# Talking-heads attention and a squared-ReLU layer: the loads of v tied to later pre-mixings, more idle multiplications early, a new order of TensorE's work

## The chip, the cores and the metric

The kernel runs on one core of a Trainium2 chip. TensorE (PE in the profile) multiplies matrices and writes PSUM; ScalarE (ACT) and VectorE (DVE) read PSUM and write SBUF; GpSimd (POOL) does some of the elementwise work and issues the loads from and the stores to device memory; SyncE (SP) issues copies from SBUF to SBUF. The metric is the device time of one execution in microseconds, the median of several runs; smaller is better.

## The reference

Eight batches of 12 heads, 448 positions, head dimension 64. Scores of all heads are mixed across heads before the softmax, the probabilities are mixed across heads again after it, and the result goes through a two-layer network with relu squared:

```python
scores = scale * np.matmul(q, k.transpose(0, 1, 3, 2))
scores = np.einsum('bhij,hg->bgij', scores, w_pre)
scores = scores - np.max(scores, axis=-1, keepdims=True)
attn = np.exp(scores)
attn = attn / (np.sum(attn, axis=-1, keepdims=True) + 1e-09)
attn = np.einsum('bhij,hg->bgij', attn, w_post)
attn_out = np.matmul(attn, v)                      # 8 x 12 x 448 x 64
x = attn_out.transpose(0, 2, 1, 3).reshape(8 * 448, 768)
out = np.square(np.maximum(x @ w_in, 0.0)) @ w_out # 768 -> 2048 -> 768
```

The kernel takes the softmax without subtracting the maximum; the scores of these inputs are small.

## The kernel before, in words

Each batch goes through a pipeline, and the pipelines of neighbouring batches overlap.

- **Loads.** q and k of the next batch come in twelve DMAs of 112 KB (`load_qk`, line 659), v of a batch in six DMAs of 128 KB (`load_v`, line 670). POOL issues them, in one queue with its own elementwise work and the stores of results.
- **Transposes** (`emit_T`, line 762): q and k are turned on TensorE and put into `qkt`.
- **Scores** (`emit_QK`, line 905): a batch has four tiles of query rows, 128 rows each and 64 in the last. A unit of TensorE work multiplies for one pair of heads (for two pairs in the last tile, whose units are numbered 0, 2, 4); ACT and DVE copy each result from PSUM into `stage`. `stage` has two buffers, so a tile's copies wait until all of the tile two before it has been moved out of its buffer.
- **Moves** (`emit_rel`, line 951): SP sends rows of `stage` to `dring`, ten query rows with all 12 heads (120 partitions) to a slot. This brings the heads of one query row together in the partition dimension. There are 16 slots; a batch has 46 of these chunks. A slot is free when the pre-mixing of its old chunk is done.
- **Pre-mixing** (`emit_pre`, line 974): one unit mixes two chunks over the heads by a small weight matrix. ACT takes the exponential into `pring` (line 991, with row sums), DVE the reciprocal (1005), POOL folds it into the second mixing's weights (`wk2s`, 1012) and into a piece of the probabilities (`ptail`, 1027).
- **Post-mixing** (`emit_post`, lines 1057 and 1072): mixes again and transposes at once; ACT and DVE copy into `a2t`.
- **AV** (`emit_AV`, line 1138): the product with v in two halves of the query rows; it needs all six loads of v. Its result `xt` feeds F1 (`emit_F1`, 1217; 1189 for batches 0 and 1), relu and square (1245, 1246, 1255), and F2 (`emit_F2`, 1334; 1283 for the last tiles), whose results POOL stores (1366).

Of batch 0 the first 240 query rows take another way, without moves (lines 835 and 861).

What runs when is settled at build time by a planner (`_Plan.run`). TensorE's order is written out by hand as the string `ORDER`: each digit takes the next unit of one of ten streams (0 transposes, 1 QK, 2 pre-mixing, 3 post-mixing, 4 AV, 5 the way of batch 0, 6 and 7 F1, 8 and 9 F2). The other engines' orders come out of the planner, which takes ready tasks by assumed costs. A load takes a pair of numbers (`dma=("load", 870.0, 60.0)`: an assumed length, and an assumed measure of how far it holds up a move), used by the planner only. A load may also be tied by `after` to a task: the planner gives it out no sooner than that task. No semaphore comes of it: on the chip POOL issues the load when it has done what stands ahead of it in its own order.

Early in the program the planner also fills gaps of TensorE with multiplications whose result nobody reads (`warm_up`, line 628): for each gap it foresees, it puts in as many as fit into a share `WSHARE` of the gap (at the very start into another share).

The ties of v before:

```python
after = [qk_tasks[(1, 2)][-1]] if b < 1 else [pre_at(b * NCP + 8 + 2 * n)]
```

`n` counts the six loads, `NCP` is 46, `pre_at` gives the pre-mixing of a chunk. So the first load of a batch is tied to the pre-mixing of its chunk 8, the last to that of chunk 18. The loads of q and k are tied to chunks 2, 4, ... 24 of the batch before theirs.

Of the kernel before, what the change touches and what calls it, by code (L numbers as in the profile page):

```python
# [25 lines left out]
DMA_END = {"move": 3700.0, "load": 2300.0}  # L26
INF = float("inf")
ORDER = (
    "0011000011000011100000000000000005550000155001531515551555335553335533255003555001335214"
    "2142114123367372262366623331721716233776331167137242244321167611376632137772226632676217"  # L30
    "7333392293093902181238213832444026702181008111813381318312772266622316267117733633262422"
    "3443317711622676311761300276223833832281383127771266730027622008338111811183324242239119"
    "3319113922291933392432422443191161136220072371263363362126711773376220063732722008118113"
    "8221819333911393119224422281833381338222444422163161173372261163733370220611637327220062"
    "1637337229010911391319222818331831182224422933931393139122442248111812433812286313630027"
    "3272263363732173621637212763362007317022091391119133922244422181183338111833822281444382"
    "2286136373227600617117163336372217622673370022882118383009313911193119222444229139131933"
    "1922283811833382224442226361713736222671376131671373362126721379223938338219938382224442"
    "2868338367686376736722276776738338444867667767676677679989998898899"
)  # L40


# [302 lines left out]
def bass_talking_heads_attention__then__ffn_squared_relu_kernel(  # L345
# [38 lines left out]
    NCP = NCH + 1  # L384
# [7 lines left out]
    with ExitStack() as es:  # L392
# [12 lines left out]
        NWP = 4  # L405
        NSUB = 2
        WARM = 60000
        WSHARE = 0.6
        WPRIO = -700.0
        WC = FH  # L410
        ident = sb("ident", [128, 128], DT.bfloat16)
# [204 lines left out]
        def warm_up(gap):  # L616
            now = plan.free[PE]
            if now > WARM or not t_warm.done:
                return
            n = int((gap - 100.0) * (0.42 if now < 6000.0 else WSHARE) / 190.0)  # L620
            if n < 1 or plan.find(1, now)[0] > now + gap:
# [27 lines left out]
        qk_tasks, v_of, av_of, f1_of, f2_of = {}, {}, {}, {}, {}  # L649
# [16 lines left out]
        def load_v(b, u, h0, deps, after, prio):  # L666
            def fn(eng, en):
                i_ = bass.AP(v.tensor, (b * H + h0) * S * D + u * (NT - NS) * D,
                             [[NT * D, PJ], [S * D, 4], [1, NS * D]])
                eng.dma_start(vraw[64 * u:64 * u + 64, h0:h0 + 4, 1 - u:1 - u + NS, :],  # L670
                              i_).then_inc(sem_v.handle, 16)

            return plan.add("ldv%d_%d_%d" % (b, u, h0), POOL, fn, deps, {POOL: (610.0, 0.0)},
                            prio, sem_v, 16, after=after,
                            dma=("load", 870.0, 60.0))

        w_of = {}
        chain = {"t": None}
# [45 lines left out]
        def emit_load_v(b):  # L724
            ts = []
            for n, (h0, u) in enumerate((h0, u) for h0 in range(0, H, 4) for u in range(2)):
                after = [qk_tasks[(1, 2)][-1]] if b < 1 else [pre_at(b * NCP + 8 + 2 * n)]
                ts.append(load_v(b, u, h0, [last_av.get(b - 1)], after,
                                 -701.0 if b == 0 else b * 1000.0 - 1600.0))
            v_of[b] = ts  # L730

        def pre_at(g):
            return pre_of[g - g % NCP + g % NCP // 2 * 2]
# [644 lines left out]
        for b in range(B):  # L1378
# [29 lines left out]
            if b == 0:  # L1408
                emit_load_w(1, [dir_done[c] for c in range(ND)])
                emit_load_v(b)  # L1410
            else:
                emit_load_v(b)
# [85 lines left out]
```

## Time and profile before

| | |
|---|---|
| median of three runs | 530.37 us (529.73 to 532.08) |
| the profiled execution, its own time | 527.85 us |
| its span on the core | 526.0 us |
| TensorE busy | 506.4 us |
| ACT, DVE, POOL busy | 436.6, 405.5, 265.3 us |
| moves from `stage` to `dring` | 365 DMAs |
| loads of v | 48 DMAs of 128 KB |

The page gives busy time by engine, the span in 40 slices, the DMA queues, the chain of work that ended last, and groups of instructions. The trace answers narrower questions: windows of time, waits by releaser, the instructions of one tile, the timeline. A busy TensorE in the profile is not TensorE at its peak, since the ends of matmuls are modelled; its idle time is the surer reading.

### The profile page before, as it was taken

The page shows a single profiled execution, that of the slowest core. Times are in us where ns is not written, and L with a number is a line of the kernel's source. Part 1 is how long each engine was busy: PE and PEld are TensorE (multiplying, and loading weights), DVE is VectorE, ACT ScalarE, POOL GpSimd, SP SyncE. Part 2 cuts the span into 40 slices and gives each one's busy share as a digit, 9 for nine tenths or more (in the row PEclk, how much of TensorE's full clock was granted, in tenths as well). Part 3 has the DMA queues.
Part 4 walks back from the last instruction along what each step waited for, and adds up shares of the span by engine and source line. Part 5 has one row for each costly group of instructions (what it writes and reads, how often), then busy time and mean ns, then how long its engine had stood idle before and what let it go on. Part 6 is the DMA issues. An engine that isn't in the chain of part 4 may idle for free.

```text
span 526.0 us, 22045 instructions
## 1 busy us (share of the span) xinstructions
PE 506.4 (96%) x8923; PEld 314.1 (60%) x8923; DVE 405.5 (77%) x1066; ACT 436.6 (83%) x1248; POOL 265.3 (50%) x571
## 2 busy tenths in 40 slices
PE   8999989999989997999979999999999999999997
PEld 3456666667756653566535665566556665568874
DVE  7989977889979787977967779986797668965440
ACT  4999988899999897989979999997889888966421
POOL 9937449335843494246643478335843356242100
PEclk9999999999999999999989999999999999999999
DMA  8999989757975699447974679646974567453004
GB/s 112 207 223 196 205 162 185 174 107 143 175 179 107 143 174 192 84 91 157 170 150 79 129 154 197 136 78 143 186 143 98 129 136 141 86 99 78 4 19 103
DMA packets 83064, 72.02 MB, mean 137 GB/s; under 512 B 7572, under 2 KB 80468, under 8 KB 82964
## 3 DMA queue, kind: packets, MB, share of 16 engines
q0 software_dynamic: 37632, 33.83, 39.9%
q1 hardware_dynamic: 45044, 36.59, 30.2%
q8 instruction: 72, 1.18, 0.9%
q10 hardware_dynamic: 288, 0.20, 0.1%
q14 instruction: 28, 0.23, 0.1%
HBM read 47.22 MB, written 11.01 MB: 111 GB/s over the span
## 4 chain that ended last, share of the span: by engine, by line
PE 67%; DMA 12%; ACT 9%; DVE 7%; SPq 2%; POOL 2%; issue 1%; ACTq 0%; DVEq 0%; POOLq 0%
PE ps L1334 21%; PE ps L1217 18%; DMA dring<-stage 10%; PE ps L974 6%; PE ps L1189 5%; PE ps L1138 5%; ACT pring L991 5%; PE ps L1057 5%; PE ps L905 4%; DVE stage L482 3%; PE ps L1283 2%; SPq L951 2%; DMA kraw<-in_k_dram 2%; ACT stage L481 1%; PE ps L762 1%; DVE a2t L482 1%
## 5 line engine op out<-in xcount | busy, mean ns | idle before, releaser
L991 ACT ACTIVATE pring<-ps 128x448 bf16<-128x448 f32 x360 | 192.8, 572 | 7.6 <-PE ps L974 6.4
L1334 PE MATMUL ps<-w_out_sb,h2t 64*128 64x384 bf16 x1664 | 151.6, 323 | 0.3 <-DVE a2t L482 0.3
L1012 POOL TENSOR_TENSOR wk2s<-wk2b,rinv 128x120 bf16<-128x120 bf16 (+1 forms) x179 | 70.8, 396 | 141.8 <-DVE rinv L1005 140.7
L482 DVE CAST a2t<-ps 128x420 bf16<-128x420 f32 (+1 forms) x201 | 121.2, 639 | 18.2 <-PE ps L1072 17.3
L1217 PE MATMUL ps<-xt,w_in_sb 64*128 64x448 bf16 (+2 forms) x1344 | 123.2, 325 | 3.4 <-ACT stage L481 2.9
L482 DVE CAST stage<-ps 128x448 bf16<-128x448 f32 (+1 forms) x180 | 107.5, 614 | 24.5 <-DMA dring<-stage 12.9
L481 ACT ACTIVATE a2t<-ps 128x420 bf16<-128x420 f32 (+1 forms) x167 | 100.6, 662 | 17.3 <-PE ps L1072 16.7
L481 ACT ACTIVATE stage<-ps 128x448 bf16<-128x448 f32 (+1 forms) x180 | 94.9, 562 | 18.5 <-PE ps L905 10.6
L1334 PEld LDWEIGHTS ps<-w_out_sb,h2t 64*128 64x128 bf16 x1664 | 77.1, 94 | 50.2 <-issue 2.0
L1217 PEld LDWEIGHTS ps<-xt,w_in_sb 64*128 64x128 bf16 x1344 | 61.3, 94 | 43.2 <-ACT stage L481 3.1
L991 ACT ACTIVATION_READ_ACCUMULATOR pring<-ps 128x1 f32 x360 | 85.4, 237 | 0.0
L1366 POOL DMA_DIRECT2D out_dram<-osb x52 | 33.5, 648 | 100.7 <-ACT pring L991 43.4
L1027 POOL TENSOR_TENSOR ptail<-pring,rinv 128x128 bf16<-128x128 bf16 x171 | 70.3, 411 | 0.0
L1057 PEld LDWEIGHTS ps<-wk2s,pring 60*128 60x128 bf16 x2160 | 47.1, 94 | 25.3 <-issue 2.7
L1057 PE MATMUL ps<-wk2s,pring 60*128 60x60 bf16 x2160 | 54.3, 187 | 2.1 <-POOL ptail L1027 0.7
L1255 DVE TENSOR_TENSOR h2t<-h1t 128x448 bf16<-128x448 bf16 (+2 forms) x176 | 55.0, 340 | 1.4 <-ACT h1t L1245 1.0
L905 PE MATMUL ps<-qkt 64*128 64x448 bf16 (+1 forms) x360 | 50.2, 354 | 5.9 <-DVE h1t L1246 2.6
L974 PE MATMUL ps<-dring,wk 64*64 64x448 bf16 (+1 forms) x672 | 54.0, 365 | 1.9 <-ACT pring L991 1.1
L1246 DVE TENSOR_SCALAR h1t<-ps 128x448 bf16<-128x448 f32 (+2 forms) x92 | 43.7, 482 | 13.6 <-PE ps L1217 9.8
L1245 ACT ACTIVATE h1t<-ps 128x448 bf16<-128x448 f32 (+2 forms) x84 | 38.2, 466 | 11.6 <-PE ps L1217 10.0
L1005 DVE RECIPROCAL rinv<-rowsum 128x2 f32<-128x2 f32 (+1 forms) x184 | 28.5, 155 | 22.3 <-ACT pring L991 21.2
L1138 PEld LDWEIGHTS ps<-a2t,vraw 128*64 128x64 bf16 x960 | 38.8, 109 | 7.0 <-ACT osb L481 2.7
(66 smaller groups left out, 534.5 us busy)
## 6 DMA issues: line engine op xcount, KB each, us to landing
dring<-stage SPq DMA_DIRECT2D x307, 105.0 KB
out_dram<-osb POOLq DMA_DIRECT2D x52, 192.0 KB, 4.2
vraw<-in_v_dram POOLq DMA_DIRECT2D x48, 128.0 KB, 5.7
qraw<-in_q_dram POOLq DMA_DIRECT2D x48, 112.0 KB, 5.6
kraw<-in_k_dram POOLq DMA_DIRECT2D x48, 112.0 KB, 4.8
w_in_sb<-in_moe_w_in_dram POOLq DMA_DIRECT2D x8, 384.0 KB, 20.7
w_out_sb<-in_moe_w_out_dram POOLq DMA_DIRECT2D x8, 384.0 KB, 19.6
dring<-stage SPq DMA_DIRECT2D x30, 42.0 KB
```

What stands on the lines that cost most here:

```text
L481: return eng.activation(o, i_, AF.Copy)
L482: return eng.tensor_copy(o, i_)
L905: r_ = eng.matmul(ps[y * w:(y + 1) * w, g.banks[x], 0:S], qkt[r0:r0 + 64, pb, p + y, 0, i0:i0 + w], qkt[r0:r0 + 64, pb, p + y, 1, :], star ...
L974: r_ = eng.matmul(ps[64 * y:64 * y + 64, gr.banks[x], 0:S], wk1[64 * x:64 * x + 64 - R0 * x, :], dring[64 * x:64 * x + 64 - R0 * x, (g0 + ...
L991: return eng.activation(pring[:, pr, 0:S], ps[:, gr.banks[x], 0:S], AF.Exp, accum_out=rowsum[:, pr, :])
L1012: return eng.tensor_tensor(wk2s[:, p0:p0 + n, :], i0.to_broadcast([128, n, PR]), rinv[:, p0:p0 + n, :].to_broadcast([128, n, PR]), ALU.mult)
L1027: return eng.tensor_tensor(ptail[:, p0 // 2, :, :], pring[:, p0:p0 + 2, 0:PJ], rinv[:, p0:p0 + 2, :].to_broadcast([128, 2, PJ]), ALU.mult)
L1057: r_ = eng.matmul(ps[:, gr.banks[x], o0:o0 + PR], pring[64 * x:64 * x + PR, pr + y, (2 * k + 1) * PJ:(2 * k + 3) * PJ], wk2s[64 * x:64 * x ...
L1138: r_ = eng.matmul(po, vraw[:, h, sl, :], m, start=(k == 0), stop=(k == NS))
L1217: r_ = eng.matmul(ps[:, g.banks[x], 0:n], w_in_sb[64 * y:64 * y + 64, ft, t * 128:(t + 1) * 128], xt[64 * y:64 * y + 64, ft, c0:c1], start ...
L1255: return eng.tensor_tensor(h2t[:, t16, o0:o0 + n], h1t[:, s, 0:n], h1t[:, s, 0:n], ALU.mult)
L1334: r_ = eng.matmul(ps[:, g.banks[hh], 0:FH], h2t[64 * y:64 * y + 64, t16, col:col + 128], w_out_sb[64 * y:64 * y + 64, t16, hh * FH:(hh + 1 ...
```

## The change

Four edits. `WSHARE` goes from 0.6 to 0.85. The measure by which the planner lets a load of v hold up a move goes from 60 to 88, the number that the loads of q and k have. For batches 2 to 7 the six loads of v are tied to the pre-mixings of chunks 14, 17, 20, 23, 26 and 29 (an odd chunk stands for the pair that it is in), in place of 8, 10, ... 18; batches 0 and 1 keep theirs. And `ORDER` is another string with as many of each digit.

```diff
 ORDER = (
-    "0011000011000011100000000000000005550000155001531515551555335553335533255003555001335214"
-    "2142114123367372262366623331721716233776331167137242244321167611376632137772226632676217"
...
+    "0010000110100011010000155500000000001155355531155055500003305055300555333520055311135352"
+    "2441141233622673376262236133772111761376333127673222444213666761377111632236722677126332"
...
-        WSHARE = 0.6
+        WSHARE = 0.85
...
             return plan.add("ldv%d_%d_%d" % (b, u, h0), POOL, fn, deps, {POOL: (610.0, 0.0)},
                             prio, sem_v, 16, after=after,
-                            dma=("load", 870.0, 60.0))
+                            dma=("load", 870.0, 88.0))
...
             for n, (h0, u) in enumerate((h0, u) for h0 in range(0, H, 4) for u in range(2)):
-                after = [qk_tasks[(1, 2)][-1]] if b < 1 else [pre_at(b * NCP + 8 + 2 * n)]
+                after = [qk_tasks[(1, 2)][-1]] if b < 1 else [
+                    pre_at(b * NCP + (8 + 2 * n if b < 2 else 14 + 3 * n))]
```

No instruction of the computation is added or taken away; TensorE gets 27 idle multiplications for 23. What moves is shown at three places. Lines below the last edit have a number higher by one in the changed kernel.

**POOL in batch 4.** Rows of POOL's order from the fold of chunks 8 and 9 on (before), which bring four of the batch's six loads of v (line 670) among loads of batch 5's q and k (659) and the folds of chunks 10 to 13 (1012, 1027):

```order
L670 DMA vraw<-in_v_dram 64x4x256
L659 DMA qraw<-in_q_dram 64x2x448
L670 DMA vraw<-in_v_dram 64x4x256
L659 DMA qraw<-in_q_dram 64x2x448
L1012 TENSOR_TENSOR wk2s<-wk2b,rinv 128x120
L1027 TENSOR_TENSOR ptail<-pring,rinv 128x128
L1012 TENSOR_TENSOR wk2s<-wk2b,rinv 128x120
L1027 TENSOR_TENSOR ptail<-pring,rinv 128x128
L670 DMA vraw<-in_v_dram 64x4x256
L659 DMA kraw<-in_k_dram 64x2x448
L670 DMA vraw<-in_v_dram 64x4x256
L659 DMA kraw<-in_k_dram 64x2x448
```

Ahead of these rows stands one load of v after the fold of chunk 3, behind them the sixth after that of chunk 17. Now the first two loads of v stand behind the fold of chunks 12 and 13:

```order
L670 DMA vraw<-in_v_dram 64x4x256
L659 DMA kraw<-in_k_dram 64x2x448
L670 DMA vraw<-in_v_dram 64x4x256
L659 DMA kraw<-in_k_dram 64x2x448
L1013 TENSOR_TENSOR wk2s<-wk2b,rinv 128x120
L1028 TENSOR_TENSOR ptail<-pring,rinv 128x128
L1013 TENSOR_TENSOR wk2s<-wk2b,rinv 128x120
L1028 TENSOR_TENSOR ptail<-pring,rinv 128x128
L659 DMA qraw<-in_q_dram 64x2x448
L670 DMA vraw<-in_v_dram 64x4x256
L659 DMA qraw<-in_q_dram 64x2x448
L670 DMA vraw<-in_v_dram 64x4x256
```

The next two come after the fold of chunk 17, and the last two together after that of chunk 25. Ahead of the fold of chunk 15 stood five of the six loads before, and stand two now. The loads of q and k keep their places within a pair or two of chunks. The same holds for the other batches from 2 on; in batch 3 four of six are out by the fold of chunk 21, in batch 2 four by that of chunk 19, where all six were by 17 and 13 before. In batch 7 the last two come after the fold of chunk 25.

**TensorE at the last query tile of batch 3** (905 and 906 are the QK units, 4 matmuls each; 1217 and 1218 F1 of batch 2; 974 pre-mixing). Before, from the first QK unit of that tile on:

```order
L905 MATMUL ps<-qkt 64x448 x4
L974 MATMUL ps<-dring,wk 64x448 x4
L1217 MATMUL ps<-xt,w_in_sb 128x448 x24
L905 MATMUL ps<-qkt 64x448 x8
L1217 MATMUL ps<-xt,w_in_sb 128x448 x24
L1057 MATMUL ps<-wk2s,pring 128x60 x12
L1072 MATMUL ps<-wk2b,ptail 128x60 x2
```

The second and third unit stand together. Now, from the F1 unit ahead of the second QK unit to the third:

```order
L1218 MATMUL ps<-xt,w_in_sb 128x448 x12
L906 MATMUL ps<-qkt 64x448 x4
L975 MATMUL ps<-dring,wk 64x448 x4
L1218 MATMUL ps<-xt,w_in_sb 128x448 x24
L763 MATMUL ps<-ident,qkr 128x64 x28
L1218 MATMUL ps<-xt,w_in_sb 128x448 x12
L1058 MATMUL ps<-wk2s,pring 128x60 x12
L1073 MATMUL ps<-wk2b,ptail 128x60 x2
L1218 MATMUL ps<-xt,w_in_sb 128x448 x12
L1058 MATMUL ps<-wk2s,pring 128x60 x12
L1073 MATMUL ps<-wk2b,ptail 128x60 x2
L906 MATMUL ps<-qkt 64x448 x4
```

Between the second and the third now stand four F1 units of 12 matmuls, two transposes, a pre-mixing and two post-mixings. At the same place of batch 4 the order of the F1, QK and post-mixing units is what it was.

**TensorE at the start** (628 are the idle multiplications, 775 and 776 transposes, 835 and 836 the way of batch 0). Before, from the second group of idle multiplications on:

```order
L628 MATMUL ps<-warm 128x448 x3
L775 MATMUL ps<-ident,kraw 64x64 x28
L628 MATMUL ps<-warm 128x448
L905 MATMUL ps<-qkt 128x448 x4
L835 MATMUL ps<-qkt 32x448 x8
L775 MATMUL ps<-ident,qraw 64x64 x28
L628 MATMUL ps<-warm 128x448
L775 MATMUL ps<-ident,kraw 64x64 x28
```

Now:

```order
L628 MATMUL ps<-warm 128x448 x4
L776 MATMUL ps<-ident,kraw 64x64 x28
L628 MATMUL ps<-warm 128x448 x2
L906 MATMUL ps<-qkt 128x448 x2
L836 MATMUL ps<-qkt 32x448 x8
L776 MATMUL ps<-ident,qraw 64x64 x28
L628 MATMUL ps<-warm 128x448 x3
L776 MATMUL ps<-ident,kraw 64x64 x28
```

The three groups grow by one, one and two; a QK unit of 2 moves behind the second pair of transposes.

More of the change, by code (lines that the diff above doesn't have):

```diff
@@ L28 @@
 ORDER = (
-    "0011000011000011100000000000000005550000155001531515551555335553335533255003555001335214"
-    "2142114123367372262366623331721716233776331167137242244321167611376632137772226632676217"
[L31 to L39, printed above, removed]
+    "0010000110100011010000155500000000001155355531155055500003305055300555333520055311135352"
+    "2441141233622673376262236133772111761376333127673222444213666761377111632236722677126332"
+    "7733393912290293802381283213444200762180018111812383338316712267122266116732167337332244"
+    "4213673117612267611672330076722277383128338133832671006226722008338111811183324242239119"
+    "1119313933292229339242244324319116311622007317332622366321637127700736312672237800138122"
+    "8318119133913391192224422813833183318222424442236136173117326116733372200611637327022062"
+    "1637337229100913391119222818313833182224422933911193319322442224438113813183228631160022"
+    "7372263363372217623637211763063072372200931931191119222444223811831183138338222814443382"
+    "2287163367226116001731716333672127622637337002183821289318300911191139222444229139319333"
+    "9222818118333812244422261637133716222667337336171371612267221792183933822938339382224442"
+    "2833836768687736372226767637673384448678667676776767679989988988999"
 )
```

## The prediction

> **What bounds the kernel now.** First the page: which engine has the least idle time, and whether the clock drops.
>
> ```profile
> span 526.0 us, 22045 instructions
> PE 506.4 (96%) x8923; PEld 314.1 (60%) x8923; DVE 405.5 (77%) x1066; ACT 436.6 (83%) x1248; POOL 265.3 (50%) x571
> PEclk9999999999999999999989999999999999999999
> ```
>
> TensorE is idle for 526.0 - 506.4 = 19.6 us, some of it at the two ends, where nothing can be multiplied yet or any more. So a change that leaves the multiplications as they are can win some 15 us at most. One slice shows a lower clock.
>
> Next the end, since a stall that is taken away early is worth its length only if no other limit waits later. From 462 to 523 us:
>
> ```profile
> 462.00:523.00 61.00, 60.41 (x1010) 44.54 (x1004) 26.11 (x81) 28.23 (x83) 12.70 (x27) 1.00 0.27 59
> ```
>
> TensorE is busy for 60.4 of 61 us while ACT and DVE are idle for more than half. It has a backlog there, so a microsecond won in batches 2 to 6 reaches the end whole, and one lost does too.
>
> Third the waits of TensorE between 100 and 436 us, with total, times and longest, and the places on the timeline:
>
> ```profile
> PE ps L1217 <- ACT stage L481: 2.9, 1, 2.9
> PE ps L905 <- DVE h1t L1246: 2.6, 1, 2.6
> PE ps L974 <- ACT pring L991: 1.1, 1, 1.1
> PE ps L905 <- DVE a2t L482: 0.4, 2, 0.2
> ...
> 146.06 0.38 PE L974 MATMUL ps<-dring,wk 64*64 64x448 bf16 x4 [1.06 <-ACT pring L991]
> ...
> 206.24 0.38 PE L905 MATMUL ps<-qkt 64*64 64x448 bf16 x4 [2.63 <-DVE h1t L1246]
> 206.90 0.38 PE L905 MATMUL ps<-qkt 64*64 64x448 bf16 x4 [0.28 <-DVE stage L482]
> ...
> 266.94 2.42 PE L1217 MATMUL ps<-xt,w_in_sb 64*128 64x448 bf16 x12 [2.94 <-ACT stage L481]
> ```
>
> Three stalls, in batches 2, 3 and 4, all beside the last query tile (the units of 64 rows), make up 6.9 us; no other wait reaches half a microsecond. The named releasers, ACT and DVE, are only the last link. The chain of waits at the three places says what they waited for:
>
> ```profile
> 141.58 7.16 DMA dring<-stage
> ...
> 194.60 1.14 PE ps L1217 x12
> ...
> 196.44 8.51 DMA dring<-stage
> ...
> 259.03 6.11 DMA dring<-stage
> ```
>
> From the end of their issue these moves took 6 to 8.5 us to land. A copy into `stage` stands in ACT's and DVE's in-order queues until the tile two before is out of its buffer, so the copies behind it, which free PSUM for TensorE, stand too. The last of the three costs more than its idle time: the unit after it took 2.42 us, where the same 12 matmuls otherwise take 1.14, and the windows show why.
>
> ```profile
> 200.00:210.00 10.00, 6.95 (x88) 2.97 (x86) 6.56 (x17) 7.01 (x18) 3.89 (x8) 1.00 0.88 192
> 266.00:268.00 2.00, 1.06 (x6) 0.43 (x8) 1.94 (x4) 1.93 (x5) 0.00 (x0) 0.72 0.99 157
> 268.00:270.00 2.00, 2.00 (x26) 0.98 (x22) 0.86 (x3) 1.21 (x4) 0.00 (x0) 0.50 0.94 186
> 270.00:274.00 4.00, 4.00 (x72) 1.79 (x68) 3.42 (x10) 3.87 (x14) 1.64 (x4) 0.96 0.57 138
> ```
>
> From the means, half clock lasted 2 x 0.28/0.5 + 2 + 4 x 0.04/0.5 = 3.4 us, which loses 1.7 us of work. So batch 4's stall is worth 2.9 + 1.7 = 4.6 us. Batch 3's left the clock at 1.00.
>
> **The loads of v** (batches 2 to 7). Ten microseconds around 195, where batch 3's moves were late:
>
> ```profile
> q0 software_dynamic: 1596, 1.24, 79.2%
> vraw<-in_v_dram POOLq DMA_DIRECT2D x5, 128.0 KB, 6.5
> ```
>
> POOL's queue took 79.2% of the DMA engines for 10 us to move 1.24 MB: 7.9/1.24 = 6.4 us a MB, so a load of v (0.128 MB) is worth about 0.8 us of all 16 engines. They are taken from the moves of a tile, 13 of them, that run at the same time. By the orders shown, before its stall batch 4 now has three loads fewer to wait behind (two instead of five), batches 3 and 2 two fewer each.
>
> *Batch 4*: TensorE's order at the place is unchanged, so only the loads act. Three loads are 2.4 us of the 2.94; if that shortens the stall, the half clock should mostly go as well. I take 2.4 for the idle time and 1.0 of the 1.7, a gain of 3.4; bounds 0 (the moves wait for something else) and 4.6.
> *Batch 3*: two loads are 1.6 us, and the third QK unit now stands four F1 units (12 matmuls, 1.14 us each) further back, which by itself covers more than the 2.6 us if the wait comes at that unit. It may come at the second, so I take 2.5; bounds 0 and 2.9.
> *Batch 2*: two loads are 1.6 us against 1.06 of stall, but the order there was rewritten as well and I can't tell its slack: 0.5; bounds 0 and 1.1.
>
> [...]
>
> **What the loads meet later.** The load work isn't less, it comes 6 to 11 chunks later. These are the windows it goes into:
>
> ```profile
> 190.00:200.00 10.00, 10.00 (x206) 5.24 (x202) 9.43 (x23) 9.49 (x28) 9.61 (x20) 1.00 1.07 189
> 210.00:220.00 10.00, 10.00 (x207) 5.65 (x201) 9.20 (x26) 9.23 (x28) 2.44 (x6) 1.00 0.48 91
> ...
> 320.00:330.00 10.00, 10.00 (x184) 5.38 (x180) 9.43 (x25) 9.53 (x29) 7.80 (x17) 1.00 1.06 205
> 330.00:340.00 10.00, 10.00 (x170) 4.87 (x166) 9.87 (x26) 9.72 (x28) 3.08 (x8) 1.00 0.58 133
> ```
>
> The last numbers but one are the DMA share: 1.07 at the peak of batch 3, 0.48 and 0.58 in the stretch after the loads. Two to four loads of 0.8 us bring such a stretch to between 0.64 and 0.9, under the level at which moves were late; and batch 5 shows 1.06 with no stall at all, so a high share does not always bite. But the moves of that stretch fill the tile that the next batch's first query tile waits for. I take 2.0 us lost over the six batches, two stalls like batch 2's; bounds 0 and 9.2 (two like batch 4's).
>
> **AV** waits for the last load. Time from issue to landing of v in batches 5 to 7, and of F2's units:
>
> ```profile
> DMA to landing us min/median/max: 3.0/5.2/8.1
> ...
> 220.58 1.30 PE ps L1334 x16
> ```
>
> In batch 7, which has the least room, the last two loads follow the fold of chunk 25. From that pair's pre-mixing to AV TensorE's order has seven F2 units (9.1 us) and some 3 us of smaller ones; exponentials and fold take about 3 of the 12. The 9 that are left are more than the longest landing, 8.1. So 0; bounds 0 and 3. Behind a late AV would stand everything of TensorE.
>
> **The idle multiplications.** Four more, in gaps that the trace shows:
>
> ```profile
> 7.32 0.81 PE L628 MATMUL ps<-warm 128*128 128x448 bf16 x3
> 8.06 0.41 PE L775 MATMUL ps<-ident,kraw 64*64 64x64 bf16 x28
> ...
> 9.14 0.55 PE L905 MATMUL ps<-qkt 64*128 64x448 bf16 x4 [0.38 <-DVE qkt L482]
> ...
> 11.28 0.41 PE L775 MATMUL ps<-ident,kraw 64*64 64x64 bf16 x28 [0.45 <-DMA kraw<-in_k_dram]
> ```
>
> Three took 0.74 us from start to the next start, 0.25 each, so four are at most 1.0 us. Their cover is the wait for `qkt` (0.38) and for `kraw` (0.45); without it they cost the 1.0. The granted clock is full in this part already, so no gain. I take +0.1; bounds 0 and 1.0.
>
> **The rest of the order**, batch 0 and the places named nowhere: as many units of each kind, so 0, with bounds of 1.5 either way, a stall like batch 2's and its neighbours of 0.4 that could come or go.
>
> The sum: -(3.4 + 2.5 + 0.5) + 2.0 + 0 + 0.1 + 0 = -4.3 us. On the profiled execution, 527.85 us in all with a span of 526.0, that gives 523.5. The median of the runs, 530.37, stands 2.5 above that execution, so I forecast 530.37 - 4.3 = 526.1 us, and call anything within 0.5% of the median (527.7 to 533.0) no change, about what a measurement of this kernel can tell.
>
> **Rivals.**
> *The stalls only move* (no change). Loads and moves share the DMA engines, the work is the same, and what batches 3 and 4 win comes back at the next batch's first tile. Then the 6.4 us won are lost again: 530.4. For it: POOL's queue with 79% leaves SP's moves little while it runs. Against: the 0.48 and 0.58 above. [...]
> *The later loads collide worse* (slower). Now two loads go out together after chunk 25, while SP moves the third tile of the batch, and the order leaves the next batch's first units no more room. If half of the old gain is lost (+3.2) and two places stall by 2.9 us each, 530.4 - 3.2 + 5.8 = 533.0; where one brings half clock, 534.7. It decides as soon as the new stalls exceed 6.4 + 2.7 us, or the old ones stay and the new exceed 2.7. For it: a single stall of that sort costs 4.6. Against: the waits of 100 to 436 us name no fourth stall of half a microsecond, so the first query tiles of batches 3 to 7 have had room so far.
> *AV waits for v*: landings of 10 to 12 us in batches 2, 6 and 7 would cost 1 to 3 us each and eat the gain: 529.
> *All three stalls and the half clock go and nothing comes back*: 530.4 - 4.6 - 2.9 - 1.1 = 521.8.
>
> **How the numbers follow.** Forecast 0.47, with its own range 523.5 to 528.5; stalls only move 0.20; collide worse 0.19; AV waits 0.05; all go 0.09. The range from 520.2 to 533.8 takes in the best case, the no-change rival and the near end of the slow one, and leaves out about 0.14, mostly above. Faster by over 0.5%: 0.42 of the forecast, the 0.09, together 0.51. Slower by over 0.5%: the slow rival and a bit of the first, 0.22. The rest, 0.27, within.
>
> **What would show it.** The waits of TensorE beside batch 4's last query tile: under 1 us with the clock at 1.00 if right; still 2.9 if the loads of v weren't the cause. The chain there: moves landing in under 5 us, not 6.1. DMA share flatter, under 1.0 at the old peaks and above 0.6 ten microseconds later. Wrong, if waits for `stage` appear at the first query tile of batches 3 to 7, if AV units wait for `vraw`, or if the first 60 us grow.

## The result, and the profile after

The changed kernel took 527.22 us in the median of four runs (527.06 to 528.29), the kernel before 531.09 beside it (529.73 to 532.08, four runs). The ratio is 0.9933, with a 95% interval of 0.9904 to 0.9962: a gain of 3.9 us, where 4.3 was forecast. Medians here are of all executions of a kernel, while ratios leave out the slow ones (over 1.5% above the fastest of the same kernel), so the two need not agree. One execution of all that follow, the profiled one of the kernel with still later ties, took 1732 us and is left out everywhere.

The page of the changed kernel, the same three rows as of before:

```profile
span 526.5 us, 22062 instructions
PE 507.0 (96%) x8927; PEld 314.1 (60%) x8927; DVE 407.8 (77%) x1066; ACT 435.2 (83%) x1248; POOL 266.9 (51%) x571
PEclk9999999999999999899999999999999999999999
```

The two profiles show no gain: the spans are 526.5 and 526.0. The profiled execution of before took 527.85 us, 3.2 less than the 531.09 above, that of the changed kernel 528.29, 1.1 more than its median. So the medians carry the verdict, and the traces are read for where the stalls sit. TensorE's waits from 100 to 436 us (total, times, longest), then the places on its timeline, in brackets the idle time before the unit and its releaser:

```profile
PE ps L906 <- DVE stage L482: 2.9, 3, 2.6
PE ps L906 <- ACT h1t L1246: 1.5, 1, 1.5
PE ps L1058 <- ACT stage L481: 1.1, 1, 1.1
PE ps L1218 <- DVE stage L482: 0.7, 1, 0.7
```

```profile
166.25 0.36 PE L906 MATMUL ps<-qkt 64*128 64x448 bf16 x2 [2.58 <-DVE stage L482]
...
208.98 0.38 PE L906 MATMUL ps<-qkt 64*64 64x448 bf16 x4 [1.45 <-ACT h1t L1246]
209.92 0.57 PE L975 MATMUL ps<-dring,wk 64*64 64x448 bf16 x4 [0.56 <-ACT a2t L481]
210.43 3.89 PE L1218 MATMUL ps<-xt,w_in_sb 64*128 64x448 bf16 x24
...
268.40 1.31 PE L1218 MATMUL ps<-xt,w_in_sb 64*128 64x448 bf16 x12 [0.67 <-DVE stage L482]
...
284.42 0.34 PE L1058 MATMUL ps<-wk2s,pring 60*128 60x60 bf16 x12 [1.09 <-ACT stage L481]
```

At batch 4's last query tile (268) the idle time fell from 2.94 to 0.67 us, and the twelve F1 matmuls behind it from 2.42 to 1.31. At batch 3's (209) the stall did not go in this execution: 1.45 us stand at the tile's second QK unit, and half clock follows, with 24 matmuls in 3.89 us that take 2.43 elsewhere. A stall of 2.58 is new, at the first query tile of batch 3 (166). The chain of waits has these rows for the moves behind 166, 209 and 268; a row begins with the start of SP's issue:

```profile
159.93 5.21 DMA dring<-stage
...
200.47 7.27 DMA dring<-stage
...
261.98 3.30 DMA dring<-stage
```

For batch 3 the landing went from 8.51 to 7.27 us. For batch 4 the row is shorter than the landing: at 265.28 the chain passes over to exponentials on ACT, but the copy into `stage` on DVE waited for a move until 267.00.

```profile
267.00 0.63 DVE L482 CAST stage<-ps 64x448 bf16<-64x448 f32 x1 [0.85 <-DMA dring<-stage]
```

From 261.98 on that is 5.0 us, against 6.11 before. The windows (busy time of TensorE, its weight loads, DVE, ACT and POOL, then granted clock, DMA share and GB/s) answer to those shown of before:

```profile
190.00:200.00 10.00, 9.97 (x196) 5.51 (x194) 9.40 (x22) 9.74 (x29) 7.48 (x16) 1.00 0.83 168
200.00:210.00 10.00, 7.98 (x126) 3.83 (x122) 7.66 (x20) 7.64 (x23) 6.72 (x15) 1.00 1.00 170
210.00:220.00 10.00, 10.00 (x140) 4.83 (x139) 8.74 (x20) 7.28 (x18) 2.21 (x4) 0.83 0.63 130
...
320.00:330.00 10.00, 9.95 (x196) 5.39 (x194) 9.42 (x24) 9.56 (x28) 9.66 (x21) 1.00 1.02 184
330.00:340.00 10.00, 9.73 (x154) 4.80 (x152) 9.53 (x24) 9.21 (x27) 4.76 (x11) 1.00 0.92 182
...
462.00:523.00 61.00, 60.91 (x1038) 45.05 (x1034) 24.95 (x80) 29.62 (x89) 13.67 (x30) 1.00 0.32 70
```

The DMA share from 190 on was 1.07, 0.88, 0.48 and is 0.83, 1.00, 0.63: the crowd came ten microseconds later and is a little lower. From 320 on 1.06 and 0.58 became 1.02 and 0.92. The end is still TensorE's alone, 60.91 of 61 us.

### The profile page after: what moved, and what is told of

Its sections match the earlier page's. It is cut to its first block, busy times and chain, and to the rows that moved or that the text cites. A ratio compares the mean times of both kernels' runs of the same rounds, so it can differ in the third digit from the quotient of the medians.

```text
span 526.5 us, 22062 instructions
## 1 busy us (share of the span) xinstructions
PE 507.0 (96%) x8927; PEld 314.1 (60%) x8927; DVE 407.8 (77%) x1066; ACT 435.2 (83%) x1248; POOL 266.9 (51%) x571
## 4 chain that ended last, share of the span: by engine, by line
PE 66%; ACT 18%; DMA 10%; DVE 2%; issue 1%; POOL 1%; SPq 0%; ACTq 0%; POOLq 0%; DVEq 0%
PE ps L1335 23%; PE ps L1218 17%; DMA dring<-stage 9%; ACT pring L992 9%; PE ps L1139 6%; PE ps L975 5%; PE ps L1058 4%; PE ps L906 4%; ACT a2t L481 3%; ACT stage L481 3%; PE ps L1190 3%; PE ps L1284 2%; DVE stage L482 2%; PE ps L763 1%; DMA kraw<-in_k_dram 1%
## 5 line engine op out<-in xcount | busy, mean ns | idle before, releaser
L482 DVE CAST stage<-ps 128x448 bf16<-128x448 f32 (+1 forms) x189 | 112.4, 614 | 25.0 <-DMA dring<-stage 13.3
L482 DVE CAST a2t<-ps 128x420 bf16<-128x420 f32 (+1 forms) x202 | 120.9, 635 | 13.6 <-PE ps L1073 12.8
L481 ACT ACTIVATE a2t<-ps 128x420 bf16<-128x420 f32 (+1 forms) x166 | 101.7, 674 | 13.2 <-PE ps L1073 12.8
L481 ACT ACTIVATE stage<-ps 128x448 bf16<-128x448 f32 (+1 forms) x171 | 89.9, 561 | 21.0 <-DMA dring<-stage 10.4
L1028 POOL TENSOR_TENSOR ptail<-pring,rinv 128x128 bf16<-128x128 bf16 x171 | 71.5, 418 | 0.0
L975 PE MATMUL ps<-dring,wk 64*64 64x448 bf16 (+1 forms) x672 | 52.4, 364 | 1.7 <-ACT a2t L481 0.6
L1246 ACT ACTIVATE h1t<-ps 128x448 bf16<-128x448 f32 (+2 forms) x90 | 40.8, 465 | 15.4 <-PE ps L1218 13.8
L1247 DVE TENSOR_SCALAR h1t<-ps 128x448 bf16<-128x448 f32 (+2 forms) x86 | 41.5, 487 | 13.2 <-PE ps L1218 11.7
L1190 PE MATMUL ps<-xt,w_in_sb 128*128 128x220 bf16 (+1 forms) x384 | 42.5, 260 | 2.3 <-ACT stage L481 2.1
```

The source lines that it names most:

```text
L481: return eng.activation(o, i_, AF.Copy)
L482: return eng.tensor_copy(o, i_)
L975: r_ = eng.matmul(ps[64 * y:64 * y + 64, gr.banks[x], 0:S], wk1[64 * x:64 * x + 64 - R0 * x, :], dring[64 * x:64 * x + 64 - R0 * x, (g0 + ...
L1028: return eng.tensor_tensor(ptail[:, p0 // 2, :, :], pring[:, p0:p0 + 2, 0:PJ], rinv[:, p0:p0 + 2, :].to_broadcast([128, 2, PJ]), ALU.mult)
L1190: r_ = eng.matmul(ps[:, g.banks[0], 0:n], w_in_sb[:, ft, t16 * 128:(t16 + 1) * 128], xt[:, ft, c0:c1], start=(ft == 0), stop=(ft == NFT - 1))
```

## The experiments

Two theories stood at the start. By L the later loads of v carry the gain: fewer loads beside the moves, earlier landings. By O the new order of TensorE's work carries it, and the loads matter little. All ratios are to the kernel before, run between the others on the same chip. Its medians in the four groups of runs were 533.25, 531.09, 531.26 and 530.91.

**The changed kernel again**, with no edit, to see how firm the result is.

> The changed kernel once more, as the measure for the others. Both theories (L: the loads of v beside the moves were what cost, so the new ties bring the gain; O: the new order of TensorE brings it by the room it leaves) expect 0.993 of the kernel before, 0.990 to 0.996. A third, that the runs of before only happened to be slow, expects 0.997 to 1.000.

526.99 us, ratio 0.9897 (0.986 to 0.9933), twelve runs from 521.95 to 530.78. The gain is there again, here 6.3 us by the medians and 5.5 by the ratio. The profiled execution took 530.66 us, 3.7 above the median. TensorE's longest waits in it, from 100 to 436 us, are of a kind that the first profile of the changed kernel did not have: pre-mixing waits for its own move.

```profile
PE ps L975 <- DMA dring<-stage: 4.7, 2, 2.9
```

**The new order with the old ties.** The edit on the changed kernel:

```diff
-                    pre_at(b * NCP + (8 + 2 * n if b < 2 else 14 + 3 * n))]
+                    pre_at(b * NCP + 8 + 2 * n)]
```

> The changed kernel with the ties of v put back to every second pre-mixing from the eighth; order, planner's measure 88 and idle multiplications as changed. L: nearly all of the gain is lost, 0.997 to 1.003 of the kernel before, and the stall beside the last query tile of batch 4 is back with 2 us or more. O: most of it stays, 0.992 to 0.996, and that stall is under 1.5 us.

530.25 us, 0.997 (0.9929 to 1.0011).

**The new ties with the old order.** On the kernel before, the same line the other way round:

```diff
-                after = [qk_tasks[(1, 2)][-1]] if b < 1 else [pre_at(b * NCP + 8 + 2 * n)]
+                after = [qk_tasks[(1, 2)][-1]] if b < 1 else [
+                    pre_at(b * NCP + (8 + 2 * n if b < 2 else 14 + 3 * n))]
```

> The kernel before with the new ties of v alone; order, planner's measure 60 and idle multiplications as before. L: most of the gain is here, 0.990 to 0.995, and the stalls beside the last query tiles of batches 3 and 4 are under 1 us each. O: 0.997 to 1.003, the stalls are still 2 us or more in one of the two.

529.99 us, 0.995 (0.9917 to 0.9984). By the ratios the ties alone give 0.5% (2.7 us), the order alone 0.3% (1.6), both together 1.0% (5.5). The interval of the order alone takes in 1, and all three overlap, so the times point to both parts without settling the split. At batch 4's last query tile, where TensorE's order is the same in all of them, the rows are, with new ties and old order:

```profile
265.25 1.31 PE L1218 MATMUL ps<-xt,w_in_sb 64*128 64x448 bf16 x12 [1.64 <-ACT stage L481]
```

and with old ties and new order:

```profile
268.96 1.32 PE L1218 MATMUL ps<-xt,w_in_sb 64*128 64x448 bf16 x10 [2.73 <-ACT stage L481]
```

So there it is the ties that shorten the wait. At batch 3's last query tile, with the new ties and the old order, the wait goes from the second QK unit, where it stood before, to the third; in TensorE's waits from 100 to 436 us it is

```profile
PE ps L906 <- DVE stage L482: 2.1, 1, 2.1
```

With the old ties and the new order neither of these two units waits (206 and 209). A pre-mixing ahead of them does, for its own move, and half clock follows (0.83 granted from 200 to 210):

```profile
201.46 0.59 PE L975 MATMUL ps<-dring,wk 64*64 64x448 bf16 x4 [2.01 <-DMA dring<-stage]
...
206.36 0.36 PE L906 MATMUL ps<-qkt 64*64 64x448 bf16 x4
...
209.23 0.38 PE L906 MATMUL ps<-qkt 64*64 64x448 bf16 x4
```

**No loads of v from batch 2 on.** On the kernel before; AV of batches 2 to 7 multiplies with v of batch 1, and 36 loads of 128 KB are left out.

```diff
         def emit_load_v(b):
+            if b > 1:
+                v_of[b] = v_of[1]
+                return
```

> The kernel before without the loads of v of batches 2 to 7 (36 of 48 loads left out; AV of these batches uses the v of batch 1). It takes the suspected cost away altogether, with the order as before. L: the stalls of batches 2, 3 and 4 (6.9 us idle and 1.7 of half clock) go, 0.984 to 0.989 of the kernel before. O: the moves are late for want of room in the order, 0.994 to 0.999, with at least one of the three stalls left at 2 us or more.

523.87 us, 0.9854 (0.9809 to 0.9898). The loads of v, 36 of them, cost the kernel before 1.5%, some 8 us. Its two places on the timeline, batch 3's and batch 4's last query tile:

```profile
205.71 0.38 PE L908 MATMUL ps<-qkt 64*64 64x448 bf16 x4 [2.00 <-DVE rinv L1008]
206.02 3.20 PE L1220 MATMUL ps<-xt,w_in_sb 64*128 64x448 bf16 x16
...
264.46 1.31 PE L1220 MATMUL ps<-xt,w_in_sb 64*128 64x448 bf16 x12 [0.22 <-ACT stage L481]
```

Batch 4's wait is gone: the loads of v were its cause. At batch 3 the second QK unit no longer waits, but the third does: without a single load of v it waits 2.00 us, and half clock follows (0.50 from 207 to 209). The move behind it landed in 5.56 us, where 8.51 were shown with v:

```profile
199.36 5.56 DMA dring<-stage
```

Leaving the loads out also takes their issue from POOL, which was busy for 242.9 us in place of 265.3, and the planner's orders come out anew. These were not tried apart from the load on the DMA engines; the earlier landing speaks for the engines.

**The kernel before against itself**, twelve runs, to see what the comparison can tell.

> The kernel before, once more and with a profile of its own: 0.997 to 1.003. If the stalls sit at fixed places, its waits name the same three as the first profile (1.1, 2.6 and 2.9 us beside the last query tiles of batches 2, 3 and 4) within 1 us each. If they come and go with the landing of moves, at least one of the three is under 1 us or another place of 1 us or more appears, and an execution some 4 us longer than the first profile's shows about 4 us more of waits.

534.55 us, 1.0061 (1.0021 to 1.0101). The same kernel came out 0.6% slower than itself, and its interval leaves 1 out. So half a per cent, or 3 us, is not settled by one such comparison: the two halves of the change (0.997 and 0.995) are not shown by their times. The changed kernel's gain, 0.7 and 1.0%, has the same sign in two comparisons, and in two more below with a small edit each (0.9904 and 0.9885). This profile of before, with a span of 531.9 us against the first one's 526.0, had the waits

```profile
PE ps L1217 <- ACT stage L481: 3.4, 1, 3.4
PE ps L905 <- DVE h1t L1246: 3.2, 1, 3.2
PE ps L974 <- DMA dring<-stage: 2.8, 3, 1.6
PE ps L974 <- ACT pring L991: 1.0, 1, 1.0
```

The first two are the known places. The third is a kind that the first profile did not have: pre-mixing waits for its own move.

**No loads of v in the changed kernel**, the same edit.

> The changed kernel without the loads of v of batches 2 to 7 (AV of these batches uses the v of batch 1). If the new ties have taken away most of what v cost, it is 0 to 2 us under the changed kernel: 0.986 to 0.990 of the kernel before. If the loads of v cost as much at their new places, it is 4 us or more under it: 0.978 to 0.983.

523.04 us, 0.9861 (0.9822 to 0.99). That is as far under the kernel before as without v in the old order (0.9854). So once v is gone the new order, with its idle multiplications, gives nothing that comparisons of 0.4% either way can see; what it gains, it seems to gain against v. The loads of v cost the changed kernel 4 us by the medians (527.0 to 527.2 against 523.04), 2 to 4 by the ratios (0.9897 and 0.9933 less 0.9861): half of the 8 before, or less. The two places now:

```profile
204.63 0.38 PE L909 MATMUL ps<-qkt 64*64 64x448 bf16 x4
...
261.77 1.31 PE L1221 MATMUL ps<-xt,w_in_sb 64*128 64x448 bf16 x12 [0.19 <-DVE stage L482]
```

Neither place waits. At batch 3 it is the order that freed the third unit: the ties alone, and no v in the old order, left it waiting 2.15 and 2.00 us. With v in the kernel a pre-mixing ahead of the tile then waits for its own move in four of the six profiles with the new order and the old places of q and k: 2.01 with the old ties, 1.78 (the changed kernel's second), 2.58 and 1.48 (the old share and the mixture, below). Without v nothing waits there.

**Ties later still**, on the changed kernel:

```diff
-                    pre_at(b * NCP + (8 + 2 * n if b < 2 else 14 + 3 * n))]
+                    pre_at(b * NCP + (8 + 2 * n if b < 2 else 17 + 3 * n))]
```

> The changed kernel with v tied to every third pre-mixing from the seventeenth on, the last to chunk 32, two before the pre-mixing ahead of AV in batches 2, 6 and 7. If AV had room to spare, the same as the changed kernel within 1.5 us (0.987 to 0.993). If the margin of AV was about used up, AV units wait for loads of v, 2 us or more each in batches 2, 6 and 7, and the time is 4 to 10 us above the changed kernel (0.997 to 1.010).

540.52 us in the median of the other five, 1.0194 (1.0156 to 1.0232), a larger loss than either expectation. One more look at the same kernel, for its trace:

> The kernel with v tied to every third pre-mixing from the seventeenth on, once more, for a profile at full clock: 538 to 543 us. If AV's margin was used up, TensorE's longest waits are AV units for loads of v, 1.5 us or more each in at least three batches, and add up to 8 us or more; if the loads collide with moves instead, the waits are for copies into stage as in the others.

536.99 us. The waits of TensorE in its whole span:

```profile
PE ps L1139 <- DMA vraw<-in_v_dram: 7.2, 1, 7.2
PE ps L1139 <- ACT pring L992: 3.0, 1, 3.0
```

and their places:

```profile
409.75 4.12 PE L1139 MATMUL ps<-a2t,vraw 128*64 128x220 bf16 x60 [3.00 <-ACT pring L992]
...
476.67 4.61 PE L1139 MATMUL ps<-a2t,vraw 128*64 128x220 bf16 x60 [7.17 <-DMA vraw<-in_v_dram]
```

AV of batch 7 waits 7.17 us, AV of batch 6 3.00. The releaser that is named for the second is an exponential, but the weight loads of both, which read v, waited for v (total, times, longest):

```profile
PEld ps L1139 <- DMA vraw<-in_v_dram: 11.0, 2, 7.6
```

The change left less room than three chunks in the last two batches; in batches 2 to 5 nothing waited at AV.

**The share of idle multiplications back to 0.6** in the changed kernel:

```diff
-        WSHARE = 0.85
+        WSHARE = 0.6
```

> The changed kernel with the share of the gaps for idle multiplications back at 0.6 (and the order of the other engines as the planner then makes it). If the idle multiplications only fill gaps, the first 60 us and the whole stay within 1 us of the changed kernel (0.988 to 0.992). If they bring part of the gain, it loses 1.5 us or more (0.993 to 0.997), with a lower granted clock or longer waits before 20 us.

525.91 us, 0.9904 (0.9861 to 0.9947), beside the changed kernel's 0.9897 and 0.9933: no cost and no gain that can be told.

**Loads of q and k earlier.** If what remains is the crowd of q, k and v together, q and k of batches 3 to 7 could go into the quiet stretch of the batch before:

```diff
-                            after = [chain["t"], pre_at((b - 1) * NCP + 2 + 2 * n)]
+                            after = [chain["t"], pre_at(
+                                (b - 1) * NCP + 2 + 2 * n if b < 3 else (b - 2) * NCP + 24 + 2 * n)]
```

> The changed kernel with the loads of q and k of batches 3 to 7 tied to chunks 24 to 46 two batches ahead, in place of 2 to 24 one batch ahead: their buffer is free by then, and the DMA share there is low. v as in the changed kernel. If what v still costs (some 4 us) is the crowd of loads of q, k and v at chunks 14 to 24, it goes: 0.981 to 0.986 of the kernel before. If v costs by itself wherever moves run, or by the stores at chunks 34 to 46, the loads of q and k only meet other moves: 0.988 to 0.995.

528.84 us, 0.9962 (0.9937 to 0.9987). And with v drawn forward into the room that this makes, beside that edit:

```diff
-                    pre_at(b * NCP + (8 + 2 * n if b < 2 else 14 + 3 * n))]
+                    pre_at(b * NCP + (8 + 2 * n if b < 2 else 6 + 3 * n))]
```

> As the last one, and v of batches 2 to 7 tied to every third pre-mixing from the sixth on, where no load of q or k is left: loads spread evenly over the batch. If the crowd is what costs: 0.980 to 0.985, with no stall of 1.5 us beside the last query tiles of batches 3 to 5. If the single load hurts wherever it falls: 0.988 to 0.995, with stalls at those tiles as in the kernel before.

528.76 us, 0.9977 (0.9951 to 1.0003). Both are slower than either expectation had it, and neither beats the changed kernel's 0.9897 and 0.9933 (it was not run in this group). The first one's profile has no wait over a microsecond left at the old places, but in TensorE's waits from 100 to 436 us many small ones, for exponentials and the fold:

```profile
PE ps L1059 <- ACT pring L993: 1.6, 3, 0.6
PE ps L907 <- ACT pring L993: 1.0, 3, 0.4
PE ps L1059 <- POOL ptail L1029: 0.9, 2, 0.7
```

**A mixture**: the later ties where AV had room, the changed kernel's where it had none.

```diff
-                    pre_at(b * NCP + (8 + 2 * n if b < 2 else 14 + 3 * n))]
+                    pre_at(b * NCP + (8 + 2 * n if b < 2 else 17 + 3 * n if b < 6 else 14 + 3 * n))]
```

> The changed kernel with v of batches 2 to 5 tied to every third pre-mixing from the seventeenth, and of 6 and 7 from the fourteenth as in the changed kernel. If the later ties of batches 2 to 5 free the last query tiles further (the second profile of the later kernel has no wait over 1.3 us between 100 and 360) and only AV of batches 6 and 7 paid for them, it is 1 to 4 us under the changed kernel: 0.981 to 0.988 of the kernel before, with no AV unit waiting over 1 us for v. If that profile was only a good execution, it equals the changed kernel: 0.988 to 0.993.

525.00 us, 0.9885 (0.9842 to 0.9928), six runs from 523.47 to 527.38. It beats the kernel before; from the changed kernel (0.9897 and 0.9933) it can't be told apart.

Over all groups, the idle time of TensorE from 100 to 436 us in the profiles (336 us less its busy time in that window), beside the clock that was granted there:

| kernel | idle, us | clock |
|---|---|---|
| before, first profile and second | 9.5, 12.8 | 0.99, 0.99 |
| new ties, old order | 10.7 | 1.00 |
| old ties, new order | 10.7 | 0.99 |
| changed, first profile and second | 8.9, 11.2 | 0.99, 0.99 |
| changed, share 0.6 | 10.5 | 1.00 |
| changed, ties later still | 8.0 | 0.99 |
| q and k early, with v too | 8.3, 8.2 | 1.00, 1.00 |
| mixture | 8.8 | 1.00 |
| no v, old order | 4.9 | 0.99 |
| no v, new order | 3.1 | 1.00 |

The rows without v stand apart. Between the others two profiles of one kernel differ by 2 to 3 us, as much as the kernels do.

## Why the prediction was right, and where not

The forecast was -4.3 us and the measurement -3.9, inside the range. The terms were less good than their sum, and that the sum came so close is in part luck: in the two profiles the terms add up to nothing. In the table a half clock counts with 1.7 us, half of its 3.4.

| term of the sum | predicted | in the profiles of before and after |
|---|---|---|
| batch 4's place | -3.4 | -4.0 |
| batch 3's place | -2.5 | +0.8 |
| batch 2's place | -0.5 | -1.1 |
| what the later loads meet | +2.0 | +3.7 |
| AV | 0 | 0 |
| idle multiplications | +0.1 | 0 |
| the rest | 0 | +1.1 |
| sum | -4.3 | +0.5 (spans), -3.9 (medians) |

- **Batch 4's place** was right in cause and nearly in size. The idle time fell by 2.27 us, where 2.4 was said, and the half clock went whole, 1.7 us, where 1.0 was said: 4.0. Since TensorE's order is the same there, the waits can be put beside each other: 2.94, 3.38 (before, second profile) and 2.73 with the old ties; 1.64, 0.67, 2.15 (the changed kernel's second profile) and 0.75 (the old share) with the new; 1.09 and 1.08 with the ties of 17 (the mixture and the kernel with still later ties); 0.22 and 0.19 with no v. The last updates of the moves' semaphores give, in the same order, the median time from the start of issue to the landing for the moves begun from 254 to 264 us: 5.5, 6.6 and 6.0; 5.4, 4.8, 5.5 and 5.1; 4.5 and 4.8; 4.3 and 4.2. The 2.15 says that the gain is not the same in every execution.
- **Batch 3's place** is the step that failed. The 2.63 us were set off against the third unit, which the new order moves back, but the prediction's own rows have them at the second, with 0.28 at the third. In the changed kernel's first profile the second unit still waits: 1.45 + 0.56 idle and 1.7 of half clock make 3.7, against 2.63 + 0.28 = 2.9. That is one execution. In the five other profiles with the new order, v loaded and q and k at their old places, neither unit waits over 0.2 us, and in four of them a pre-mixing ahead waits 1.5 to 2.6 us for its own move instead. So the order did free the units, and the late moves were felt at another place. "Two loads are 1.6 us" did not hold for the third unit either: without any v the old order still waits 2.00 us there. What holds it (loads of q and k, or the order alone) was not tried apart.
- **Batch 2's place**: its wait of 1.06 us is gone from the list. ("The rest" in the table is what is left to the difference of the spans.)
- **The later loads** meet moves, as was said, at the first query tile of the next batch, but it was mis-sized: 2.58 at 166 us and 1.09 at 284 make 3.7, not 2.0. A wait for `stage` at such a tile was on the prediction's list of what would show it wrong, and this one came; that the later loads made it is argued, since no other profile has the 2.58. The kinds of victim were too few as well: pre-mixing that waits for its own move was named nowhere. It takes 4.7 us in the changed kernel's second profile, where half clock follows the longest of them (0.54 from 330 to 332), 4.0 with the old share, 2.5 in the mixture and with the old ties, and 2.8 in the second profile of before; it is in neither profile without v.
- **AV** had no wait. The landings of v in batches 5 to 7 were 3.3 to 7.1 us, under the 9 us of room that was worked out from the order; three chunks later the room was gone. The rival had the right mechanism and the margin was judged rightly.

```profile
DMA to landing us min/median/max: 3.3/5.5/7.1
```

- **Idle multiplications** cost nothing that the kernel with the old share shows. The first 60 us did not grow: TensorE was idle for 4.0 us of them, as before.
- **The step from the profile to the median** carried more than was seen. The terms were read from an execution that was 2.5 us better than the median, and the difference went in as a constant. It was stalls as well, as the second profile of before shows: 3.4 and 3.2 us at the two known places and 2.8 at pre-mixing. The stalls that the change softens are longer in the usual execution than in the one that was read. This is how medians can gain 3.9 us where the two profiles show none; it is argued from one profile, not shown by many.

Two readings of the prediction were off without changing its sum. Its 6 to 8.5 us of landing count from the start of SP's issue, not from the end. And the 12 matmuls that "otherwise take 1.14" have rows of 1.31; 1.14 is from one unit's start to the next.

Of the rivals "the stalls only move" was the nearest: up to half of what v cost is still there, at other places.

Still open: why batch 3's second unit waited in one profile of the new order and in no other, what the remaining 2 to 4 us of v are made of one by one, and why executions of one kernel differ by up to 15 us (524 to 539 for before).

## What to carry to other kernels

Loads that nobody needed yet were not free beside moves on the critical path: they cost 8 us of 531 here, of which the change won back half or more. Leave such loads out once, to see what they cost in all, before moving them about. Where stalls come from landing times, one profile is one draw: take the size of a stall from two or three, and run the kernel against itself before trusting half a per cent. When a load is put off, look for the point where its consumer waits; here three chunks of 46 separated the best place found from a loss of 1.9%.

## What was not expected of the hardware

- **Half clock did not go by the length of the gap.** In the changed kernel's first profile it came after idle times of 1.45 and 0.56 us, in that of before not after 2.63 and 0.28. The clock records of these two profiles have one stretch of half clock each inside the program, both of 3.413 us, from 209.98 on in the changed kernel and from 266.90 on in before. That is 204.80 and 259.41 us after the start of the record, 60.0 and 76.0 times the 3.413. Cut into stretches of that length from the record's start, TensorE in the changed kernel has (busy, clock, DMA share, GB/s):

```profile
162.20:165.61 3.41, 1.47 (x18) 1.00 0.51 104
...
206.57:209.98 3.41, 1.39 (x20) 1.00 0.93 178
209.98:213.40 3.42, 3.42 (x22) 0.50 0.74 154
```

and in the kernel before, at batch 3's and at batch 4's place:

```profile
202.05:205.46 3.41, 1.56 (x18) 1.00 0.95 179
205.46:208.87 3.41, 2.36 (x26) 1.00 0.70 190
...
263.49:266.90 3.41, 0.51 (x18) 1.00 0.77 148
266.90:270.31 3.41, 3.37 (x32) 0.50 0.94 178
```

The 2.63 us of before lie on both sides of 205.46, so neither stretch has more than 1.85 us of idle time. In its second profile the same wait was 3.2 us, and half clock follows (0.83 granted from 210 to 220). Over the two profiles cut in this way, half clock followed the stretches with 2.90 and 2.02 us of idle time, and none of those with 1.94 or less (the start and the end of the program left aside). That the idle time within such a stretch decides is the author's reading of these few rows; no run was made to show it. The record starts 5.18 us into the span in the changed kernel and 7.49 in before, so by this reading it is chance whether a gap of 2 to 3 us costs another 1.7 us.
- **36 loads of 128 KB cost 8 us of 531** although no unit of TensorE ever waited for v itself in the kernel before. By the estimate from the queue's row (0.8 us of all 16 engines each) they are 29 us of DMA time, so about a quarter of it came through to the end.
- **The spread of one kernel on one chip is as wide as 524.4 to 539.2 us** (before, over all groups), and a comparison of it with itself came out at 1.0061.
